# A fused linear-attention and expert kernel: a new hand-fixed instruction order for its first third, with the weight loads' planned transfer times raised

## The chip, the cores and the metric

The kernel runs on one core of one Trainium2 chip. A core has five instruction streams that matter here: TensorE (PE in the profile; its weight loads are listed apart as PEld), VectorE (DVE), ScalarE (ACT), GpSimd (POOL) and SyncE (SP). Each stream runs its instructions in the order in which the program lists them. POOL and SP also start the DMA transfers of this kernel: POOL loads inputs and weights, SP moves an intermediate to and from DRAM and stores the result. The metric is the time of one execution in microseconds of device time, lower is better; the median of three runs before the change is 970.37 us (969.55 to 971.73).

## The reference, cut to what matters

```python
def phi(x): return np.where(x > 0, x, np.exp(x) - 1.0) + 1.0
# attention: q, k, v are (8, 8, 576, 64)
kv  = einsum('bhsd,bhse->bhde', phi(k), v);  z = phi(k).sum(axis=2)
num = einsum('bhsd,bhde->bhse', phi(q), kv)
den = einsum('bhsd,bhd->bhs', phi(q), z)[..., None] + 1e-06
x   = (num / den) as (4608, 512)
# experts: w_gate (512, 8), w1 (8, 512, 1024), w2 (8, 1024, 512)
P = exp(x @ w_gate - max)
for _ in range(8):                      # Sinkhorn
    P /= P.sum(1, keepdims=True) + 1e-09
    P /= P.sum(0, keepdims=True) + 1e-09
    P *= 4608 / 8
out = sum over e of P[:, e:e+1] * (relu(x @ w1[e]) @ w2[e])
```

## The kernel before, in words

The 4608 rows of x are cut into nine groups of 512. Expert e has a first matrix w1(e) and a second matrix w2(e). In the attention part (`att`, sixteen head pairs numbered by n) inputs are loaded by POOL, ACT takes exponentials, DVE builds phi and evicts products, PE multiplies. Into this part the first layers of expert 0 are woven, group by group (`layer1`), and the eight Sinkhorn steps on DVE with one small PE product each (`sinkhorn`, lines 542 to 573). Forty-six products on a zero tile (`f_warm`, line 591) have no use in the result; they stand where PE has nothing else at the start.

From group 4 or 5 of expert 0 on, both layers are computed as two-by-two block products with seven block multiplications instead of eight (`block7` with line 811 for layer one, `unit` with line 1051 for layer two). For each expert these need combinations of blocks of the weights, made by DVE in `combos`: four tasks W from w1 (line 983) and four tasks T from w2 (line 997). Combinations of x per group (`x_blocks`, lines 727 to 732) are stored to DRAM buffers by SP and fetched again for each later expert (`x_load`, line 762). Each output piece is collected in a buffer acc; for expert 0 it is scaled by P afterwards (`scale0`, lines 899 and 901, possible once the last Sinkhorn task is done), for later experts a product is scaled and added as it leaves PSUM (line 1082 on DVE, lines 1089 and 1092 on ACT and POOL).

Weights are loaded by `load_w` (line 316, issued by POOL). There are two buffers for w1 and two for w2. Expert 0 has its w1 in four quarters and its w2 in two halves; for e of 1 and more, w1 comes as two loads of 64 partitions each (512 KB written) and w2 as one load of the whole matrix (1024 KB written). w1(1) and w2(1) may start only after a small POOL instruction (`f_gx`, line 1133) that waits until the x combinations of the first five groups are stored.

The order of all work comes from `_Plan`. Every task has an engine or a choice of engines, a planned duration, dependencies and buffers. `add` numbers the tasks from 0; a transfer is a task of its own on a single server called "dma", with a planned time and a latency, and the x loads and the stores of the x combinations are tasks of that server too. `run` puts out tasks one by one, and the program is what each engine gets in this sequence. The string `_FRONT` fixes the sequence of the first 1733 tasks: a number and a letter for the engine, p for PE, a for ACT, d for DVE, g for POOL, s for SP, m for the transfer server, n for none. After the last token the planner chooses by its own modelled times. So a token's place fixes what an engine has to do first, while on the chip every instruction starts when its semaphores allow it. The i-th instruction of an engine in the trace can be matched with the i-th token of its letter, by counting the instructions that each task issues; that is how task numbers and times are put together in the prediction.

Tasks that are named below: 48, 50, 52 are the loads of k, q, v of head pair 0; 54 to 66 its arithmetic, 58p its first product (line 414); 109, 111, 114, 116 the four quarters of w1(0); 602 to 612 the first layer-one products of expert 0 (line 685); 572, 586, 787, 845 stores of x combinations of groups 2, 4, 5 and 6; 590 is `f_gx`; 592 and 594 the halves of w1(1), 598 the whole w2(1); 1007 to 1010 the W and 1011 to 1014 the T combinations of expert 1; 1018 the first product of expert 1; 1529 and 1531 the halves of w1(2), 1535 w2(2), 1538 to 1545 the combinations of expert 2; 2060 and 2062 the halves of w1(3), 2066 w2(3).

Of the kernel before, what the change touches and what calls it, by code (L numbers as in the profile page):

```python
# [17 lines left out]
class _Plan:  # L18
# [121 lines left out]
    48s 49m 1n 2p 3p 50g 51m 4p 52g 53m 5p 6p 78g 79m 7p 8p 76g 77m 9p 10p 80g 81m 54a 11p 12p 0g 13p 14p 15p 126g 127m  # L140
    16p 17p 18p 128g 129m 19p 61n 62a 63d 130g 131m 55d 56d 154g 155m 64d 57n 108n 58p 109g 110m 20p 59a 21p 22p 89n
    90a 91d 156g 157m 23p 65p 24p 60a 66d 25p 26p 82a 111g 112m 27p 28p 83d 67p 29p 30p 68a 31p 84d 158g 159m 69p 92d
    85n 86p 70a 114g 133d 115m 71a 32p 93p 87d 33p 94d 34p 88a 182g 183m 35p 132a 36p 72p 139n 141d 95p 73d 37p 38p 96a
    39p 116g 117m 134d 74p 140a 97p 40p 75d 41p 42p 184g 185m 98a 161d 135n 136p 160a 142d 43p 186g 187m 44p 137d 143p
    99a 138d 45p 144d 46p 102p 167n 168a 210g 211m 103d 145p 47p 162d 146a 113n 119n 120g 602p 121m 169d 100p 603p 101d
    147p 212g 213m 170d 148a 163n 164p 149a 171p 165d 214g 215m 604p 172d 166a 555g 152p 605p 153d 188a 173p 150p 174a
    151d 118n 606p 106g 107m 608p 189d 601n 607a 175p 240g 241m 610p 609a 195n 197d 612p 176a 242g 243m 190d 614p 196a
    613d 244g 245m 191n 192p 177a 198d 616p 615d 123g 124m 216a 199p 193d 618p 194a 200d 617a 180p 556d 611a 201p 181d
    620p 202a 270g 271m 217d 178p 621a 122n 622p 179d 223n 224a 624p 218d 225d 619a 203p 226d 300g 301m 219n 220p 204a
    562g 205a 227p 221d 639p 222d 228d 246a 206p 641p 207d 638n 640a 104g 105m 229p 247d 642a 208p 268g 269m 643p 209d  # L150
    230a 272g 273m 253n 254a 645p 644d 298g 299m 248d 231p 647p 232a 255d 256d 328g 329m 249n 250p 648a 233a 302g 303m
    257p 251d 125n 625p 326g 327m 258d 252a 646a 236p 281n 283d 259p 237d 623p 260a 632d 282a 234p 261p 235d 649p 262a
    284d 628p 311n 312a 630d 629p 275d 263a 266p 650d 285p 274a 626p 286d 651p 267d 636a 382g 383m 304a 276d 238p 356g
    357m 313d 652a 314d 277n 278p 339n 341d 627p 279a 305d 239a 280a 340a 653p 306d 354g 355m 563d 287p 330g 331m 264p
    288a 657p 265d 384g 385m 289p 634d 358g 359m 307n 308p 290a 333d 557g 332a 315p 309d 659p 310d 654a 316d 442g 443m
    558s 559m 291a 672p 334d 412g 413m 342d 317p 292p 386g 387m 318a 658p 293d 367n 368a 319p 361d 660p 369d 320a 294p
    414g 415m 674p 667a 295d 321a 564g 343p 671n 673d 335n 336p 344d 388a 565s 566m 370d 676p 416g 417m 360a 389d 296p
    390d 496g 497m 337a 655p 362d 297a 338a 675a 345p 395n 397d 322p 346a 678p 323d 665a 347p 576d 324p 348a 661p 325d
    577g 396a 371p 677d 363n 364p 372d 679a 349a 398d 656p 444g 445m 365d 418a 440g 441m 680p 366d 663d 352p 373p 353d
    662p 374a 419d 681a 350p 375p 351d 425n 426a 682p 669d 391n 392p 376a 420d 377a 684p 393d 500g 501m 683d 498g 499m  # L160
    399p 685a 688p 468g 469m 394a 400d 453n 454a 380p 427d 401p 381d 686p 402a 428d 378p 687a 403p 379d 705p 404a 455d
    446a 421n 422p 447d 470g 471m 578d 569g 405a 429p 423d 579s 580m 689p 424d 560s 561m 430a 406p 707p 407d 567s 568m
    510n 511a 472g 473m 431p 456d 408p 690p 505g 432a 409d 704n 708a 691p 448d 706a 503d 433p 449n 450p 434a 570d 696a
    457p 451d 502a 709p 458d 435a 692p 452d 583d 459p 512d 438p 460a 693p 439d 698a 461p 475d 436p 462a 711p 437d 463a
    410p 584d 513d 585g 464p 411a 694p 700a 465d 474a 514p 504d 571g 586s 587m 466p 695p 515a 467d 710d 506n 507p 481n
    482a 572s 573m 712d 574s 575m 713p 476d 508a 509a 702a 741d 715p 581s 582m 714a 483d 516p 742d 477n 478p 517a 716d
    484d 518p 479a 717p 519a 480d 485p 718a 719p 520a 486d 590g 591n 592g 593m 521p 487p 522d 594g 595m 727p 488a 720d
    523p 489p 524d 746p 490a 743d 494p 491a 721p 744d 748p 745n 747a 495d 728p 749d 492p 750p 493d 722p 553n 737d 751a
    784d 525p 729a 738d 785g 752p 526a 735a 528d 725p 753a 754p 786d 554p 755a 739d 527n 529p 787s 788m 756p 588s 589m
    530d 842d 726p 757a 531d 843g 789s 790m 758p 760p 759a 1015s 1016m 723p 761a 762d 792p 532p 724p 740d 793a 733a  # L170
    533d 796p 763d 731a 794p 534d 766p 795a 798p 767a 768p 799a 791n 797a 800p 844d 802p 764d 845s 846m 806p 1072s
    1073m 801d 535p 772p 807a 803d 769a 810p 536d 773a 812p 765d 804p 537d 813a 808p 776p 809a 811a 770p 805a 816p 850p
    817d 774p 851a 777d 771a 814p 596n 1007d 818p 775d 538p 778p 819a 815d 854p 820d 779a 856p 849n 855a 539d 852p 821d
    857a 864p 1008d 826p 865a 822d 853a 866p 900d 824p 540d 901g 860p 825a 870p 827a 828p 867a 871a 830p 861d 874p 902g
    831a 858p 875d 868p 859d 834p 869a 823d 862p 1009d 541p 876p 863a 835d 872p 908p 873d 958g 832p 909a 542d 877a 836p
    833d 829a 878d 910p 837a 912p 911a 922p 879d 907n 913a 914p 959d 882p 543d 915a 923a 924p 918p 925a 928p 883a 884p
    929a 919d 916p 885a 880d 926p 960d 920p 917d 930p 961s 962m 921a 888p 963s 964m 1010d 927a 931d 544p 932p 889a 903s
    904m 966p 933d 905s 906m 892p 967a 881d 934p 545d 847s 848m 893d 972p 935a 890p 546d 973a 886p 968p 887a 970p 969a
    894p 936d 891d 547p 976p 895a 548d 980p 965n 971a 977d 974p 981a 940p 937d 975d 986p 549d 942p 987a 941a 984p 943a
    982p 978p 983a 946p 938d 990p 947a 550p 944p 985a 551d 979a 552d 950p 939d 736a 988p 991d 1018p 896a 948p 951d 780a  # L180
    989d 992p 730a 952p 949d 1528n 1529g 1530m 1019a 1020p 732g 953a 1024p 1006n 1021a 1000p 1025a 734g 1026p 1022p
    1028p 699g 1017n 1023a 998p 1029d 993a 668a 666d 597n 598g 599m 999p 781d 635a 1531g 1532m 1030p 1004d 1001p 1031a
    631g 703d 1032p 1034p 840g 1033a 994p 945d 1005a 637d 1038p 897g 995p 1039a 1027d 1035a 633d 996p 1002a 600n 1011d
    1040p 1036p 1012d 1042p 1037a 1075p 1043d 664a 1077p 1013d 997p 1076a 1078a 1041d 1044p 670a 1014d 1081p 1129s
    1130m 1045a 1083p 1003a 1079p 1046d 1050p 1082a 1047d 1052p 1048d 1051a 1074n 1080a 1055p 1053d 1054d 1085p 1049d
    1058a 1060p 838a 1086d 1059g 1063p 697d 1062d 1061d 1087p 1065d 1089p 955d 1091p 1090a 1066p 1092a 1088a 1095p
    1067d 1097p 1084d 1096a 1093p 1068d 1099p 1094a 782d 1132p 1100d 701a 1134p 1098d 1069p 1133a 1135a 1064d 1101p
    1056a 1071d 1138p 1070d 1102a 1186s 1187m 1057g 1140p 1139a 1103d 1136p 1107p 1104d 1109p 1105d 1108a 1112p 1111d
    1110d 1142p 1106d 1113a 1117p 1131n 1137a 1143d 1120p 1119d 1533n 1538d 1144p 1118d 1146p 1141d 1148p 1147a 1123p
    1149a 1145a 1152p 1124d 1154p 1125d 1153a 1150p 1122d 1156p 1155d 1151a 1189p 1157d 1191p 1190a 1121d 1126p 1192a  # L190
    1158p 1128d 1195p 1127d 1159a 1243s 1244m 1197p 1115a 1160d 1193p 1196a 1164p 1161d 1188n 1194a 1166p 1162d 1165a
    1163d 1169p 1168d 1167d 1199p 1170a 1539d 1174p 1171g 1200d 1177p 1175d 1114g 1176d 1201p 1198d 1203p 1202a 899d
    1205p 1204a 954d 1180p 1178d 1206a 1179d 1209p 1182d 1211p 1181d 1210a 1207p 1213p 1208a 1246p 1214d 1248p 1247a
    1212d 1183p 1249a 1172a 1215p 1185d 1173g 1252p 1184d 1216a 1300s 1301m 1254p 1253a 1116g 1217d 1250p 1221p 1218d
    1223p 1222a 1219d 1226p 1225d 1220d 1256p 1229a 1224d 1231p 1245n 1251a 1230g 1257d 1227a 1234p 839g 1233d 1258p
    1236d 1260p 957g 1232d 1259a 1262p 1540d 1261a 1237p 1263a 841g 1266p 1255d 1268p 1267a 1239d 1264p 1238d 1270p
# [29 lines left out]
def kernel(  # L226
# [28 lines left out]
    add = S_.add  # L255
# [50 lines left out]
    def load_w(ten, nm, pl, pieces, e, prio, deps=(), shape=None):  # L306
        g = S_.grp(pl)
        ts_ = []
# [4 lines left out]
        for part in pieces:  # L313
            for sl, off, ap in part:
# [3 lines left out]
                ti = add(("pool", 0.8), fn, acq=[gsw], use=[g, gsw], prio=prio, deps=[tal, w_part.get(nm) if ts_ else None])  # L318
# [891 lines left out]
```

## Time and profile before

| | |
|---|---|
| median of three runs | 970.37 us (969.55 to 971.73) |
| the profiled execution's own time | 969.86 us |
| its span, first to last instruction | 967.8 us |
| PE busy | 952.0 us, 98% of the span, 8576 products |
| DVE busy | 780.3 us, 81% |
| ACT busy | 578.9 us, 60% |
| POOL busy | 184.7 us, 19% |
| mean granted TensorE clock | 0.996 |
| DMA mean | 116 GB/s |

The span is cut by the page into 40 slices of 24.2 us. "Idle before" is the time in which an engine had nothing to run ahead of an instruction, and the arrow names what ended it. A wait for several things is put down to the one that came last. A DMA is listed where it is issued, and its landing is known from the semaphore that it raises.

### The profile page before, as it was taken

The numbers are of one execution on the slowest core, as the hardware profiler recorded it, in microseconds if no ns is written. First come the engines' busy times: TensorE is split into PE (matmuls) and PEld (weight loads), VectorE is DVE, ScalarE is ACT, GpSimd is POOL, SyncE is SP. The second block draws the span as 40 slices with busy tenths as digits, with TensorE's granted clock in tenths as the row PEclk, the third lists the DMA queues.
The fourth block names the chain that finished last, engine by engine and source line by source line (L and its number), as shares of the span: only waits on it lengthen the run. The fifth ranks groups of instructions, "written<-read, shape, count | busy, mean of one in ns | idle before, by whom it ended". The sixth has DMA issues, their size and how long they took to land.

```text
span 967.8 us, 21113 instructions
## 1 busy us (share of the span) xinstructions
PE 952.0 (98%) x8576; PEld 805.4 (83%) x8576; DVE 780.3 (81%) x1476; ACT 578.9 (60%) x1029; POOL 184.7 (19%) x238
## 2 busy tenths in 40 slices
PE   8999999999999999999999999999999999999998
PEld 4565578678888888888888888888888888888886
DVE  6899899588888788878887888878887888877775
ACT  6899756645555555555555555555555555555553
POOL 6653201401312011111112111111112111111110
PEclk9999999989999999999999999999999999999999
DMA  9999442522253622272226322272226322235554
GB/s 229 242 249 250 121 153 94 79 85 77 77 121 91 151 77 78 79 161 77 75 69 132 102 75 71 74 162 76 76 75 140 102 77 77 78 99 163 165 162 111
DMA packets 45681, 112.52 MB, mean 116 GB/s; under 512 B 4368, under 2 KB 25616, under 8 KB 45584
## 3 DMA queue, kind: packets, MB, share of 16 engines
q1 hardware_dynamic: 21056, 75.57, 23.7%
q0 software_dynamic: 24128, 35.07, 19.3%
q8 instruction: 67, 1.10, 0.5%
q10 hardware_dynamic: 400, 0.52, 0.2%
q14 instruction: 30, 0.25, 0.1%
HBM read 119.69 MB, written 17.69 MB: 142 GB/s over the span
## 4 chain that ended last, share of the span: by engine, by line
PE 78%; DMA 2%; DVE 0%; issue 0%; ACT 0%; ACTq 0%
PE ye L1051 33%; PE hq L811 22%; PE R L811 11%; PE Zye L811 6%; PE Zye L1051 6%; DMA w<-in_moe_w_dram 1%; DMA xs<-xd 1%; PE ye L933 1%; PE yc L917 0%; DVE h L849 0%; ACT st L1089 0%; DVE T L997 0%; DVE acc L1082 0%; DVE acc L922 0%; ACTq L1089 0%
## 5 line engine op out<-in xcount | busy, mean ns | idle before, releaser
L1082 DVE SCALAR_TENSOR_TENSOR acc<-ye,P_sb,acc 128x256 f32<-128x256 f32 x620 | 268.5, 479 | 124.5 <-PE ye L1051 122.8
L811 PEld LDWEIGHTS <-W 128*128 128x128 f16 x2144 | 210.2, 98 | 25.3
L1051 PEld LDWEIGHTS <-S 128*128 128x128 f16 x1984 | 194.1, 98 | 22.5
L1092 POOL TENSOR_TENSOR acc<-acc,st 128x256 f32<-128x256 f32 x124 | 88.1, 730 | 626.0 <-ACT st L1089 608.7
L1051 PE MATMUL ye<-T,S 128*128 128x256 f16 x1488 | 192.8, 273 | 0.0
L811 PEld LDWEIGHTS <-w 128*128 128x128 f16 x1608 | 157.5, 98 | 25.2 <-issue 5.3
L1051 PEld LDWEIGHTS <-h 128*128 128x128 f16 x1584 | 155.3, 98 | 18.4
L846 ACT ACTIVATE h<-hq 128x512 f16<-128x512 f32 x134 | 80.1, 598 | 140.5 <-PE hq L811 136.1
L811 PE MATMUL hq<-xs,W 128*128 128x256 f16 x1008 | 151.7, 273 | 0.0
L811 PE MATMUL R<-xs,W 128*128 128x256 f16 x1008 | 151.7, 273 | 0.0
L811 PE MATMUL hq<-xs,w 128*128 128x256 f16 x1008 | 141.5, 273 | 5.0 <-DVE h L849 4.9
L843 ACT ACTIVATE h<-Zye 128x512 f16<-128x512 f32 x134 | 80.1, 598 | 39.3 <-PE Zye L811 39.3
L826 ACT COPY Zye<-hq 128x512 f32<-128x512 f32 x134 | 77.7, 580 | 36.8 <-PE hq L811 36.8
L1089 ACT ACTIVATE st<-Zye,P_sb 128x256 f32<-128x256 f32 x124 | 53.0, 471 | 70.9 <-PE Zye L1051 70.9
L1022 DVE TENSOR_TENSOR S<-h 128x1024 f16<-128x1024 f16 x124 | 86.0, 694 | 11.1 <-ACT h L846 11.1
L849 DVE CUSTOM_DVE_ANT_0 h<-R,s 128x512 f16<-128x512 f32 x126 | 86.5, 687 | 9.5 <-ACT s L833 9.0
L833 ACT COPY s<-hq 128x512 f32<-128x512 f32 x126 | 73.6, 584 | 33.9 <-PE hq L811 33.2
L849 DVE CUSTOM_DVE_ANT_0 h<-hq,s 128x512 f16<-128x512 f32 x126 | 86.7, 688 | 8.0 <-PE hq L811 7.9
L811 PE MATMUL Zye<-xs,w 128*128 128x256 f16 x504 | 76.1, 274 | 0.0
L840 ACT COPY s<-R 128x512 f32<-128x512 f32 x126 | 74.7, 593 | 0.0
L1051 PE MATMUL ye<-w,h 128*128 128x256 f16 x528 | 69.2, 274 | 0.0
L1051 PE MATMUL Zye<-w,h 128*128 128x256 f16 x528 | 68.4, 272 | 0.0
(126 smaller groups left out, 1011.7 us busy)
## 6 DMA issues: line engine op xcount, KB each, us to landing
xs<-xd SPq DMA_DIRECT2D x63, 896.0 KB, 4.6
kin<-in_k_dram POOLq DMA_DIRECT2D x15, 576.0 KB, 8.4
out_dram<-acc SPq DMA_DIRECT2D x67, 128.0 KB, 2.4
w<-in_moe_w_dram POOLq DMA_DIRECT2D x16, 512.0 KB, 8.7
w<-in_moe_w_dram POOLq DMA_DIRECT2D x7, 1024.0 KB, 13.0
qin<-in_q_dram POOLq DMA_DIRECT2D x16, 288.0 KB, 8.3
vv<-in_v_dram POOLq DMA_DIRECT2D x16, 288.0 KB, 8.2
xd<-acc SPq DMA_DIRECT2D x5, 512.0 KB, 5.1
```

What stands on the lines that cost most here:

```text
L811: nc.tensor.matmul(dst[:, p, :], lhsT=lhs(p, c), rhs=rhs(c), start=(first and p == 0 and c == 0), stop=(c == 1), skip_group_check=True)
L826: nc.scalar.copy(out=Zt[1], in_=gX["tile"])
L833: nc.scalar.copy(out=gs2["tile"], in_=gX["tile"])
L840: nc.scalar.copy(out=gs5["tile"], in_=gR["tile"])
L843: nc.scalar.activation(out=hd(0, 0), in_=Zt[1], func=AF.Relu)
L846: nc.scalar.activation(out=hd(1, 0), in_=gX["tile"], func=AF.Relu)
L849: nc.vector._custom_dve(TENSOR_ADD_SAT, out=dst, in0=ps, in1=sb, s0=3.0e38, s1=0.0)
L1022: nc.vector.tensor_tensor(out=Sx[:, i], in0=a0, in1=a1, op=op)
L1051: nc.tensor.matmul(bank(g_)[:, s, :], lhsT=lhs(s, kk), rhs=rhs(kk), start=(new and s == 0 and kk == 0), stop=(kk == 3), skip_group_check=True)
L1082: nc.vector.scalar_tensor_tensor(out=dst(), in0=bank(g_)[:, s, :], scalar=P_sb[:, gg, e:e + 1], in1=dst(), op0=ALU.mult, op1=ALU.add)
L1089: nc.scalar.mul(out=gst["tile"], in_=bank(g_)[:, s, :], mul=P_sb[:, gg, e:e + 1])
L1092: nc.gpsimd.tensor_tensor(out=dst(), in0=dst(), in1=gst["tile"], op=ALU.add)
```

## The change

Two things are edited. In `load_w` the planned transfer time of one load becomes 1.55 us instead of 1.4 for a quarter of w1(0), stays 2.6 us for half a w1 and for half of w2(0), and becomes 5.4 us instead of 2.6 for a whole w2. And `_FRONT` is replaced by another sequence of 1725 tokens of the same tasks. 83 tasks that stand in both sequences stand on another engine; no task of PE, SP or a load is among them. The computation, the tiles, the buffers and the dependencies are the same, and the file still counts stores on the server of the loads, as it did.

The main moves in the new sequence: 598g (w2(1)) stands straight behind 590g and ahead of 592g and 594g, where it stood behind both of these and nine further POOL tasks: five of x combinations, three of scaling and the first half of w1(2); 594g stands behind three x combinations on POOL (842g, 844g, 901g); 1531g stands in group 4 of expert 1, 1535g in group 1 of expert 1; the combinations of expert 2 (1538d to 1545d) start in group 5 of expert 1 instead of group 1; 586s stands behind 787s; the four quarters of w1(0) and 52g stand earlier, 63d stands behind 55d and 56d. The order of POOL from `f_gx` to w2(2), in tokens:

```
before: 590 592 594 785 843 901 902 958 1529 732 734 699 598 1531 631 840 897 1059 1057 1171 1114 1173 1116 1230 839 957 841 1287 898 1228 1285 1342 1535
after:  590 598 592 842 844 901 594 958 637 957 701 699 1529 898 839 633 1059 666 780 664 896 840 1114 1116 955 841 1535
```

The diff, cut to the lines with tokens that are spoken of:

```diff
-    48s 49m 1n 2p 3p 50g 51m 4p 52g 53m 5p 6p 78g 79m 7p 8p 76g 77m 9p 10p 80g 81m 54a 11p 12p 0g 13p 14p 15p 126g 127m
-    16p 17p 18p 128g 129m 19p 61n 62a 63d 130g 131m 55d 56d 154g 155m 64d 57n 108n 58p 109g 110m 20p 59a 21p 22p 89n
...
-    99a 138d 45p 144d 46p 102p 167n 168a 210g 211m 103d 145p 47p 162d 146a 113n 119n 120g 602p 121m 169d 100p 603p 101d
...
-    484d 518p 479a 717p 519a 480d 485p 718a 719p 520a 486d 590g 591n 592g 593m 521p 487p 522d 594g 595m 727p 488a 720d
...
-    817d 774p 851a 777d 771a 814p 596n 1007d 818p 775d 538p 778p 819a 815d 854p 820d 779a 856p 849n 855a 539d 852p 821d
...
-    1028p 699g 1017n 1023a 998p 1029d 993a 668a 666d 597n 598g 599m 999p 781d 635a 1531g 1532m 1030p 1004d 1001p 1031a
-    631g 703d 1032p 1034p 840g 1033a 994p 945d 1005a 637d 1038p 897g 995p 1039a 1027d 1035a 633d 996p 1002a 600n 1011d
-    1040p 1036p 1012d 1042p 1037a 1075p 1043d 664a 1077p 1013d 997p 1076a 1078a 1041d 1044p 670a 1014d 1081p 1129s
...
-    1110d 1142p 1106d 1113a 1117p 1131n 1137a 1143d 1120p 1119d 1533n 1538d 1144p 1118d 1146p 1141d 1148p 1147a 1123p
...
+    48s 49m 1n 2p 3p 52g 53m 4p 50g 51m 5p 6p 78g 79m 7p 8p 76g 77m 9p 10p 126g 127m 54a 55d 11p 12p 80g 81m 13p 14p
+    128g 129m 56d 108n 109g 110m 57n 58p 0g 15p 130g 131m 16p 17p 18p 19p 20p 21p 61n 62a 63d 154g 155m 22p 23p 24p 25p
...
+    138a 144d 44p 160a 102p 210g 211m 145p 103d 113n 602p 146a 45p 162d 46p 47p 100p 119n 167n 120g 168a 169d 121m 603p
...
+    787s 788m 528d 756p 586s 587m 755a 789s 790m 735a 722p 757a 738d 554p 588s 589m 729a 527n 529p 723p 739d 530d 1015s
+    1016m 724p 740d 531d 758p 760p 759a 725p 761a 762d 792p 532p 794p 793a 590g 533d 597n 598g 599m 726p 763d 795a 731a
+    591n 592g 593m 796p 764d 733a 798p 534d 842g 800p 799a 766p 802p 767a 806p 791n 797a 768p 801d 807a 803d 535p 770p
...
+    1073m 810p 777d 818p 815d 774p 819a 900d 811a 850p 538p 820d 901g 778p 851a 775d 856p 779a 539d 864p 857a 594g 595m
...
+    831a 868p 875d 862p 596n 1007d 834p 863a 823d 827a 876p 1008d 869a 541p 858p 835d 908p 958g 832p 859d 909a 877a
...
+    948p 1010d 1018p 949d 992p 1019a 989d 1020p 635a 952p 1024p 600n 1006n 1011d 1021a 1000p 953a 1025a 1026p 957g 631a
+    1022p 1028p 993a 701g 998p 1017n 1029d 1023a 1027d 1001p 699g 1030p 1005d 1032p 1528n 1529g 1530m 1012d 1034p 1033a
...
+    1152p 1125d 1154p 1124d 1534n 1535g 1536m 1153a 1150p 1141d 732a 1156p 1057g 1189p 1151a 1157d 1191p 1190a 1121d
...
+    1233d 1260p 782d 954g 1262p 1261a 1237p 1263a 1259a 1266p 1531g 1532m 1239d 1268p 1238d 1267a 1264p 1235d 838a
...
+    1371d 1348p 1369d 1346d 1372p 1347d 1374p 1349d 1373a 1376p 1533n 1538d 1375a 1351p 1539d 1377a 1380p 1350d 1352d
...
+    1618p 2062g 2063m 1595d 1620p 1615d 1622p 1621a 1597p 1623a 1619a 1626p 1599d 1628p 1598d 1627a 1624p 1629d 1630p
...
-                ts_.append(add(("dma", (1.4 if nm == "w1" and len(pieces) > 1 else 2.6)), lambda _: None, deps=[ti],
+                ts_.append(add(("dma", 1.55 if nm == "w1" and len(pieces) > 1 else 2.6 if nm == "w1" or len(pieces) > 1 else 5.4), lambda _: None, deps=[ti],
```

## The prediction

> **What bounds the kernel now.** I read the page first, then the waits of PE, then the stretches of time in which PE is not full, and last the order of instructions around the largest wait.
>
> ```profile
> span 967.8 us, 21113 instructions
> ...
> PE 952.0 (98%) x8576; PEld 805.4 (83%) x8576; DVE 780.3 (81%) x1476; ACT 578.9 (60%) x1029; POOL 184.7 (19%) x238
> ...
> PE   8999999999999999999999999999999999999998
> ...
> PEclk9999999989999999999999999999999999999999
> ```
>
> PE is the bound nearly everywhere. The sequence of products is the same work before and after, so the change can only act on PE's idle time (967.8 - 952.0 = 15.8 us, of which about 4 us are the last eviction and store after PE's end) and on the one slice where the granted clock is not full, the eighth. The waits of PE over the whole span:
>
> ```profile
> PE hq L811 <- DVE h L849: 4.9, 2, 4.5
> PE kv_ps L414 <- DVE t L399: 1.5, 1, 1.5
> PE hq L685 <- DMA w<-in_moe_w_dram: 1.3, 2, 0.8
> ```
>
> One wait of 4.5 us is the largest by three times. The sequence of instructions around it, and the chain that ended last, which begins there with the transfer:
>
> ```profile
> 193.87 0.69 DVE L997 TENSOR_TENSOR T<-w 128x1024 f16<-128x1024 f16 x1 [6.42 <-DMA w<-in_moe_w_dram]
> 194.60 0.69 DVE L997 TENSOR_TENSOR T<-w,T 128x1024 f16<-128x1024 f16 x1
> 195.21 0.68 DVE L849 CUSTOM_DVE_ANT_0 h<-hq,s 128x512 f16<-128x512 f32 x1
> 195.81 0.68 DVE L997 TENSOR_TENSOR T<-w 128x1024 f16<-128x1024 f16 x1
> 195.94 1.01 PE L811 MATMUL hq<-xs,w 128*128 128x256 f16 x4 [4.54 <-DVE h L849]
> ```
>
> ```profile
> 183.29 10.56 DMA w<-in_moe_w_dram
> ```
>
> PE waits for DVE's h (token 1043), h stands on DVE behind two T combinations (1011, 1012), and the first of these waits 6.42 us for w2(1), issued by POOL at 183.29 (598) and landed 10.56 us later. The name in PE's wait is DVE, the cause is a late load. The clock beside it (columns: stretch, length, PE busy, granted clock, DMA share, GB/s):
>
> ```profile
> 190.00:192.00 2.00, 1.40 (x9) 1.00 1.11 158
> 192.00:194.00 2.00, 0.00 (x0) 1.00 1.08 196
> ...
> 196.00:197.00 1.00, 1.00 (x6) 0.50 0.00 0
> ...
> 199.00:200.00 1.00, 1.00 (x7) 0.50 0.97 409
> ...
> 201.00:202.00 1.00, 1.00 (x11) 1.00 0.06 16
> ```
>
> After the wait PE runs at half clock until about 200.9, and counts as busy.
>
> **Part 1, w2(1) moved ahead of w1(1).** In the new order 598 is the first load behind `f_gx` (590). `f_gx` waits for the stores of the first five groups. It ran at 107.7; now the store 586 of group 4 stands on SP behind 787, which was issued at 122.0, so `f_gx` comes at about 122.4 + 2.8 (landing of a store issued there) = 125.3. A w2 issued with no other weights in flight took 9.47 us (1535 at 266.16), so w2(1) lands near 136, while 1011 stands behind products that ran at 178.7. The margin is 40 us. The 4.54 us go. What is late next there: the products at 183.0 followed their h by 0.65 us, which is no wait.
>
> The clock loss: the five product groups between 195.94 and 200.92 (1044, 1081, 1083, 1079 and the first of line 1051) took 0.81, 0.85, 0.86, 0.85 and 1.61 us; at full clock the first four take 0.436 and the last 0.873. That is 4.98 - 2.62 = 2.36 us, gone with the wait, since gaps of up to 1.50 us at the start left the clock at 1.00. The Trainium skill, page "TensorE: Matmul & The Clock Gate", section "Part 1: The HAM clock gate", says the array drops to half rate after an idle window of about 3.4 us and needs about as long of busy work to recover. By it the loss would be 3.4/2 = 1.7 us, an estimate from that page, and the sum 0.66 us smaller; the trace shows about 5 us of half clock, and the row decides.
>
> **Part 2, the start.** PE's idle time before 180 is 1.32 (first instruction) and then 1.50 + 0.47 + 0.23 + 0.24 + 0.50 + 0.17 + 0.28 + 0.24 + 0.85 + 0.07 + 0.67 + 0.29 = 5.51 us, from the gap of every product group. The idle-time products on zeros, 13.3 us in all, stay 46. Three of these gaps have an answer in the new order:
>
> - 1.50 at the first product (58): DVE had 63, which waited 4.14 us for q, ahead of 55 and 56. Now 55 and 56 come first (ready at 4.5 + 1.16 + 0.76 = 6.5) and v is issued first, at 1.65, and lands when q did, at 7.21. The thirteen fill products ahead end at 1.32 + 5.2 = 6.5, so 0.7 remain: 0.8 saved. q now lands at 8.6, and its transpose is expected at about 11.5 against 11.0, so the fill products cover that.
> - 0.50 and 0.85 at the first w1(0) products (602, 606). Loads land one after the other here, 1.4 us each (14.37, 15.73, 17.18). The quarters move from place 10, 12, 14, 16 among POOL's loads to 8, 11, 14, 15, so the second and the fourth land 1.4 to 2.4 us earlier, while PE's own work ahead of 602 and 606 shrinks by 0.8 and 0.4: both gaps go, 1.35 saved.
>
> Together 2.15 us. Bounds: all of the 5.51 could go, and nothing could.
>
> **Part 3, the tasks that change engines.** Eleven x combinations go from POOL to DVE and seven the other way, first-layer evictions eleven to DVE and eight to ACT, and so on, 83 in all. Added up with each instruction's own duration (the median row of its kind where it changes engine), up to the first product of expert 1 (1018) DVE has 170.7 us instead of 168.4, ACT 145.2 instead of 145.1, POOL 61.7 instead of 64.9. The cover is DVE's idle time, 11.4 us between 40 and 180, but between 120 and 170 it is only 2.3 us of 50, and 1.3 of the 2.3 us added fall behind the first product of group 4 of expert 0. Lower bound 0 (hidden in the idle time), upper bound 2.3 as PE time. I take 1.3, because DVE is nearly full just there and feeds PE within 0.1 to 1 us at many places.
>
> **Part 4, w1(1) goes back.** With `f_gx` at 125.3 the halves are issued at about 126.5 (592) and, behind 842, 844 and 901 on POOL, at about 142 (594). Before, they landed at 113.7 and 116.2. The first user, W (1007), ran at 139.2 and now stands behind product 862 (149.6 before). Both hang on 900d: on POOL 901 (1.48) and 594 with its landing (5.6 as the first halves took) give 7.1 us; on DVE 820, 775, 539, 902, 821, 540, 822, 861, 873, 875 give 7.7 us. The load is 0.6 us ahead: cost 0, with bounds below. Queued behind 590 on POOL are also 842 and 844; 842 may then end at 129.4 and 844 near 131.5, as before (131.9 on DVE), and the store 845 and the x load 1072 on SP follow then, for a product at 189.5. x load 1015 now meets w2(1) on the DMA engines; its user comes 45 us later.
>
> **Part 5, expert 1 and later.** w2(2) goes from 266 to about 212 and the second half of w1(2) from 184 to about 240, each alone. The combinations of expert 2 press into the last 45 us of expert 1: three W more than before, 3 x 0.6 = 1.8 us of DVE, against 50 - 41.06 = 8.9 us idle per 50 us there. Four more scalings on POOL (15 for 11, 1.57 us each) lie in its idle time. Cost 0 while DVE keeps that idle time; without it, up to 1.8 us. w1(3) and w2(3) no longer meet an x load together (at 308.97 that took 10.08 us instead of 4.45, and PE waited 0.12): 0.12 saved. The raised 5.4 us acts behind the front only through POOL's place for w2 of later experts, and PE has no wait there to gain or lose: 0.
>
> **Sum.** On the profiled execution: 969.86 - 4.54 - 2.36 - 2.15 + 1.3 - 0.12 = 961.99. The median of the runs is 0.51 above that execution, so **962.5 us**. A change within 0.2% (1.9 us) can hardly be told from none.
>
> **Rivals.**
> - *B, the new front loses elsewhere.* DVE's added work turns into waits in full (2.3), the start saves nothing, and combinations of expert 2 cost 1.8: 970.37 - 7.02 + 4.1 = 967.5, and 965.4 where half of it is true. For it: DVE at 9.3 to 9.8 us of 10 between 120 and 170. Against it: ACT and POOL are free to lag.
> - *C, all start gaps go and DVE hides its work.* 970.37 - 7.02 - 5.51 = 957.8; 960.9 is where it meets the forecast. Against it: several of these gaps are waits between neighbours (PE on DVE and back) of 0.2 to 0.5 us.
> - *D, slower: the second half of w1(1) is the new late load.* In place of T, W (1007) stops DVE at about 148, with everything behind it. If 594 takes 12.98 us to land, as the longest quarter in the crowded start did, it is 6.8 us late; PE then loses about 6.8 and 2.36 of clock: 962.5 + 9.2 = 971.7, and 973.8 if the start saves nothing either. There it is slower by 0.2% from a landing time of 11.5 us on (7.02 - 1.3 + 1.94 - 2.36 = 5.3 us late, and 5.6 + 0.6 in time); the 12.03 of 1531 was with w2 in front. For 594 only an x load can be in flight. The Trainium skill, page "DMA: Bandwidth & Descriptors", section "Queues, rings and completion order", says each DMA engine takes turns packet by packet between the queues that have work. By that rule an x load of SP in flight would halve the rate of 594; the 10.08 us of the x load at 308.97 agrees with sharing.
> - *E, the change doesn't do what it says.* w2(1) is still late because `f_gx` is: that needs 40 us more than the 18 that I allow. Or another input of expert 1 is late at the same place, so that PE stops as before: about 970.
>
> **How the numbers follow.** The forecast, 960.9 to 964.3, has a chance of 0.59, B (964.3 to 968.4) 0.19, C 0.09, D 0.09, E 0.04. 962.5 is the middle of the first. The range 960.2 to 967.6 leaves out D, E, most of C and the end of B, some 0.2. Faster by more than 0.2% are the forecast, B and C, 0.87; the same are E and, with a start that saves, 0.02 of D, together 0.06; the rest of D is slower, 0.07.
>
> **What would show it.** In the changed profile: w2(1) issued near 125 and landed by 140; no wait of T (line 997) on a DMA; no wait of PE over 1.5 us behind the start, and the granted clock at 9 in the eighth slice (Part 1). PE's wait at line 414 near 0.7 and at line 685 on w gone (Part 2). DVE's waits small and PE's on DVE between 120 and 180 summing to about 1.3 (Part 3). No wait of W (line 983) on a DMA (Part 4). No wait in 200 to 330 (Part 5). Wrong would make it a wait of line 983 on w, or PE gaps on DVE of several us behind 120.

## The result and the profile after

The changed kernel takes 964.54 us, the median of seven runs (963.9 to 967.64); the kernel before, run beside it, takes 970.37 us (969.55 to 972.65, seven runs). The ratio is 0.9939, with a 95% interval of 0.9925 to 0.9953. The forecast was 962.5 us. The profiled execution of the changed kernel happens to be its longest, 967.64 us, so its trace shows more loss than a usual run has; a second profile of the same kernel (965.11 us, experiment 2) is read beside it.

From the page of the changed kernel: span, busy time, and PE's clock in 40 slices.

```profile
span 965.6 us, 21108 instructions
...
PE 950.3 (98%) x8576; PEld 805.2 (83%) x8576; DVE 782.0 (81%) x1474; ACT 579.3 (60%) x1031; POOL 184.6 (19%) x238
...
PEclk9999999999999999999999999999999999999999
```

The dip of the clock in the eighth slice is gone. The span is 2.1 us shorter: 1.7 us less PE busy time (952.0 to 950.3) and only 0.4 us less waiting. To see why the waiting hardly fell, the waits of PE (what it waited for, us in total, times, longest):

```profile
PE kv_ps L413 <- DMA vv<-in_v_dram: 3.4, 2, 1.9
PE R L556 <- DVE gs L551: 1.9, 1, 1.9
...
PE kv_ps L413 <- DVE xT L498: 1.2, 1, 1.2
```

The wait of 4.5 us for h has left the head of this list, and the waits for w at the first w1(0) products have left the list. (Code lines stand one lower than before: 997 is 996, 811 is 810, 685 is 684, 414 is 413.) A wait for `gs`, the input of the second small Sinkhorn product, has grown from 0.3 to 1.9 us, and one of 1.2 us for `xT` is new. The study turned on these two. By place, PE waited in us:

| PE idle time, us | 1.4 to 36 | 36 to 120 | 120 to 180 | 180 to 210 | later |
|---|---|---|---|---|---|
| before | 4.55 | 0.74 | 0.29 | 4.54 | 0.44 |
| changed, first profile | 5.54 | 2.23 | 1.95 | 0 | 0.44 |
| changed, second profile | 3.38 | 2.76 | 1.96 | 0 | 0.44 |

At the place of the old stall, DVE's instruction T, in the timeline of the changed kernel (start, duration, engine, line, operation, out and in, idle time before and what ended it), has 0.95 us of idle time ahead of it that is put down to its own issue; its load had landed 47 us earlier, at 136.37:

```profile
183.88 0.69 DVE L996 TENSOR_TENSOR T<-w 128x1024 f16<-128x1024 f16 x1 [0.95 <-issue]
```

And PE around the new wait for `gs` (columns: stretch, length, PE busy, granted clock, DMA share, GB/s), with the stretch of the old stall as the last line:

```profile
128.00:130.00 2.00, 0.63 (x5) 1.00 1.00 380
130.00:131.00 1.00, 0.42 (x3) 1.00 1.14 180
131.00:132.00 1.00, 1.00 (x5) 0.54 1.04 144
...
133.00:134.00 1.00, 1.00 (x6) 0.50 1.23 204
...
180.00:205.00 25.00, 25.00 (x200) 1.00 0.26 59
```

The old stall is gone entirely, clock included. A smaller copy of it, a wait of 1.95 us and 3.41 us of half clock (131.07 to 134.49, which costs about 1.7 us), now stands at 130. What made PE wait there is on two engines at once. DVE, then POOL, in the timeline:

```profile
126.88 3.16 DVE L549 TENSOR_TENSOR wt<-P_sb,Rr 128x288 f32<-128x288 f32 x1
130.07 0.45 DVE L551 TENSOR_REDUCE gs<-wt 128x8 f32<-128x288 f32 x1
```

```profile
125.68 1.56 POOL L315 DMA_DIRECT2D w<-in_moe_w_dram  x2 [0.36 <-issue]
127.25 1.17 POOL L726 TENSOR_TENSOR xst<-xT 128x512 f16<-128x512 f16 x1
128.37 1.16 POOL L727 TENSOR_TENSOR xst<-xT 128x512 f16<-128x512 f16 x1
```

DVE is not queueing there: one instruction of 0.67 us (the median of the eight at this line) lasts 3.16 us, and it ends at 130.04, 0.5 us after the second of the two TENSOR_TENSORs of task 842 on POOL (129.53). That gave a theory which the prediction did not have: DVE instructions are held up by POOL's x combinations. The rival is the prediction's own reason, that DVE has too much work. The two ask for opposite edits.

### The profile page after: what moved, and what is told of

Same layout as the page of the kernel before. It is cut to its first block, busy times and chain, and to the rows that moved or that the text cites. A ratio compares the mean times of both kernels' runs of the same rounds, so it can differ in the third digit from the quotient of the medians.

```text
span 965.6 us, 21108 instructions
## 1 busy us (share of the span) xinstructions
PE 950.3 (98%) x8576; PEld 805.2 (83%) x8576; DVE 782.0 (81%) x1474; ACT 579.3 (60%) x1031; POOL 184.6 (19%) x238
## 4 chain that ended last, share of the span: by engine, by line
PE 95%; DMA 2%; DVE 2%; issue 0%; ACT 0%; POOL 0%; DVEq 0%; ACTq 0%; POOLq 0%
PE ye L1050 36%; PE hq L810 24%; PE R L810 12%; PE Zye L810 6%; PE Zye L1050 6%; PE ye L932 4%; PE hq L684 3%; DMA vv<-in_v_dram 2%; PE kv_ps L413 1%; PE att L439 1%; PE att L470 1%; PE num_ps L470 1%; DVE wt L549 0%; PE att L515 0%; PE yw L590 0%
```

## The experiments

Experiments 1 to 4 ran on one chip beside the kernel before (971.36 us, median of eleven runs), experiments 5 to 8 on another beside it again (970.74, median of 29).

### 1. The kernel before, with w2(1) alone moved

```diff
-    484d 518p 479a 717p 519a 480d 485p 718a 719p 520a 486d 590g 591n 592g 593m 521p 487p 522d 594g 595m 727p 488a 720d
+    484d 518p 479a 717p 519a 480d 485p 718a 719p 520a 486d 590g 591n 592g 593m 521p 487p 522d 594g 595m 597n 598g 599m
...
-    1028p 699g 1017n 1023a 998p 1029d 993a 668a 666d 597n 598g 599m 999p 781d 635a 1531g 1532m 1030p 1004d 1001p 1031a
+    1026p 1022p 1028p 699g 1017n 1023a 998p 1029d 993a 668a 666d 999p 781d 635a 1531g 1532m 1030p 1004d 1001p 1031a
```

> The kernel before with one change: the load of w2(1), tokens 597n 598g 599m, stands behind 595m, straight behind both halves of w1(1); nothing else is moved. Theory L (the late load is the whole gain): the T combinations wait for no DMA, PE's 4.54 us wait at line 811 and the 2.36 us of half clock go, and the rest of the new order is worth nothing or costs: 970.4 - 6.9 = 963.5, at most 964 and below the changed kernel. Theory R (the new order as a whole brings it): with the old order around it another input of expert 1 is late next, PE still stops for 1 us or more between 180 and 205, and the time is 965 to 969.

Measured: 963.51 us (961.9 to 964.67, six runs), ratio 0.9915 (0.9898 to 0.9932). w2(1) was issued at 112.61 and landed at 125.16. The head of PE's waits, and DVE where it stopped before:

```profile
PE kv_ps L414 <- DVE t L399: 1.9, 1, 1.9
PE hq L685 <- DMA w<-in_moe_w_dram: 1.7, 2, 1.1
```

```profile
188.85 0.89 DVE L901 TENSOR_SCALAR acc<-acc,P_sb 128x512 f32<-128x512 f32 x1
189.67 0.68 DVE L997 TENSOR_TENSOR T<-w 128x1024 f16<-128x1024 f16 x1
```

T follows its neighbour without a wait, the wait for h is not at the head of the list, PE does not wait at all between 180 and 210, and the mean granted clock is 1.0 instead of 0.996. One load in another place gives 7.85 us (6.6 to 9.9 by the interval); Part 1 had 6.9. It is also more than the whole change gave: no run of it was as long as the shortest run of the changed kernel in experiment 2. So the other moves of the new order, with the load early, cost something.

### 2. The changed kernel once more

No edit.

> The changed kernel once more, for a second profile beside the others. The profile shown was its slowest of seven runs (967.64 against a median of 964.54). Expected: 964.5 again; in the profile the wait for v at 7.9, about 1.6 at 27.7, 1.2 at 95 and 1.9 at 130.6 again, since they come from the order. If the half clock of 3.4 us behind 131 is missing here, it is what parts the slow runs from the others (1.7 us).

Measured: 965.94 us (965.07 to 966.54, six runs), ratio 0.9942 (0.9925 to 0.9959), the same as the first time within the intervals. The wait of 1.96 us for `gs` is there again, at 129.7, but this time PE runs on at full clock. So that wait is a property of the order, and the half clock behind it is not in every run. The wait of 1.18 us for `xT`, at 94.4, also comes again; DVE and then POOL ahead of it:

```profile
90.89 2.76 DVE L450 TENSOR_SCALAR tq<-qin 128x1152 f16<-128x1152 f16 x2
93.57 0.74 DVE L498 TENSOR_TENSOR xT<-num_ps,rden 128x576 f16<-128x576 f32 x1
```

```profile
90.24 1.15 POOL L727 TENSOR_TENSOR acc<-xT 128x512 f16<-128x512 f16 x1
91.34 0.72 POOL L380 DMA_DIRECT2D kin<-in_k_dram  x1
92.08 1.25 POOL L729 TENSOR_TENSOR acc<-xT,acc 128x512 f16<-128x512 f16 x1
```

Two TENSOR_SCALARs last 2.76 us together, beside the x combinations of tasks 583 and 584 and a DMA issue between these, and the eviction of `xT` stands behind them.

### 3. Task 842 on DVE

```diff
-    591n 592g 593m 796p 764d 733a 798p 534d 842g 800p 799a 766p 802p 767a 806p 791n 797a 768p 801d 807a 803d 535p 770p
+    591n 592g 593m 796p 764d 733a 798p 534d 842d 800p 799a 766p 802p 767a 806p 791n 797a 768p 801d 807a 803d 535p 770p
```

> The changed kernel with task 842 (x combinations of group 6, first part) on DVE instead of POOL, in the same place. Theory P (POOL at work stretches a DVE instruction of some forms): the DVE instruction wt<-P_sb,Rr at line 549 near 127 falls from 3.16 us to below 1.2, PE's wait of 1.95 us for the second Sinkhorn product falls below 0.5 although DVE has 0.7 us more to do, and the time is 1.5 to 3 us below the changed kernel, 961.5 to 963. Theory O (DVE has too much in that place): wt stays long or the wait grows by 0.7 us, and the time is 964.5 to 966.

Measured: 962.91 us (961.37 to 964.31, six runs), ratio 0.9909 (0.9892 to 0.9926), 3.0 us below experiment 2. DVE in the timeline:

```profile
126.29 0.67 DVE L549 TENSOR_TENSOR wt<-P_sb,Rr 128x288 f32<-128x288 f32 x1
126.99 0.45 DVE L551 TENSOR_REDUCE gs<-wt 128x8 f32<-128x288 f32 x1
```

DVE was given more to do and was done sooner: the instruction takes 0.67 us, PE waits for nothing between 120 and 180, and DVE's busy time in the whole span falls from 782.1 (experiment 2) to 779.5 us, because the time that an instruction is held up counts as busy. The theory that DVE has too much work asked for the opposite, and falls for this place. Of the 3.0 us the trace explains 1.96 as the wait; the rest may be half clock in the unprofiled runs, whose mean clock is 0.997 to 0.999 in experiment 2 and 0.999 or 1.0 here, but no trace of those runs shows where.

### 4. Tasks 583 and 584 on DVE

```diff
-    448d 429p 423a 472g 473m 424a 686p 430d 405a 583g 406p 687d 705p 453n 454a 407d 431p 691p 455d 432a 468g 469m 510n
-    512d 511a 408p 584g 433p 409d 707p 434a 698d 470g 471m 449n 450p 704n 708a 456d 505g 706d 689p 451a 435a 513d 457p
+    448d 429p 423a 472g 473m 424a 686p 430d 405a 583d 406p 687d 705p 453n 454a 407d 431p 691p 455d 432a 468g 469m 510n
+    512d 511a 408p 584d 433p 409d 707p 434a 698d 470g 471m 449n 450p 704n 708a 456d 505g 706d 689p 451a 435a 513d 457p
```

> The changed kernel with tasks 583 and 584 (x combinations of group 4) on DVE instead of POOL, in the same places. Theory P: the two DVE instructions of line 450 near 92 and 93 fall from 1.45 and 1.40 us to 0.46, PE's wait of 1.19 us at the product of head pair 13 (line 413) falls by half or more although DVE has 1.2 us more: time 0.3 to 1 us below the changed kernel. Theory O: the wait grows by the added work, 2 us or more, and the time is 965 or more.

Measured: 964.16 us (962.76 to 966.46, six runs), ratio 0.9925 (0.9908 to 0.9943), 1.8 us below experiment 2, though the ranges overlap. The same two TENSOR_SCALARs in the timeline:

```profile
92.44 0.82 DVE L450 TENSOR_SCALAR tq<-qin 128x1152 f16<-128x1152 f16 x2
```

From 2.76 us to 0.82, and the wait for `xT` fell from 1.18 to 0.12 us. The mechanism is the same at a second place, with another kind of DVE instruction. (POOL's DMA issues move too, and end ahead of the TENSOR_SCALARs here; where such an instruction met a DMA issue alone it was 0.32 us longer at most, as the last section says.) The profile is that of the longest run. The wait for `gs`, which this edit does not touch, stands in it with 1.95 us up to 129.61, and 3.41 us of half clock follow it; the same stretch of half clock stands at 8.07, at the end of a wait of 2.53 us for v.

### 5. All three tasks on DVE

The edits of experiments 3 and 4 together, on the changed kernel.

> The changed kernel with 583, 584 and 842 all on DVE. If POOL's work beside DVE is the cause of both waits, the two gains add up: PE has neither the wait of 1.2 us near 95 nor that of 1.95 us near 130, and the time is 1 to 1.5 us below the kernel with 842 alone on DVE (962.9 there): 961.4 to 962. If DVE is by then full, it is 963 or more.

Measured: 961.17 us (960.37 to 962.08, four runs), ratio 0.9907 (0.9894 to 0.992). This is faster than both kernels: its interval lies below that of the change (0.9925 to 0.9953), and no run of it is as long as the shortest run of the changed kernel (963.9). From experiment 3 alone (0.9909) it can't be told apart. Its largest waits of PE:

```profile
PE kv_ps L413 <- DMA vv<-in_v_dram: 1.8, 1, 1.8
...
PE att L470 <- ACT rden L483: 0.8, 2, 0.6
```

These lie in the start. Not all of the mechanism is gone: at 52.57 a TENSOR_SCALAR of line 450 takes 2.04 us instead of 0.45 beside a TENSOR_TENSOR of POOL (53.11 to 54.28), as one does in the changed kernel. PE has 0.60 us of idle time shortly behind it, which the profile puts down to a load of v here and to DVE in the changed kernel. DVE is busy for 778.9 us, 3.2 less than in experiment 2, with five instructions more.

### 6. The start of before, the rest as changed

```diff
-    48s 49m 1n 2p 3p 52g 53m 4p 50g 51m 5p 6p 78g 79m 7p 8p 76g 77m 9p 10p 126g 127m 54a 55d 11p 12p 80g 81m 13p 14p
+    48s 49m 1n 2p 3p 50g 51m 4p 52g 53m 5p 6p 78g 79m 7p 8p 76g 77m 9p 10p 80g 81m 54a 11p 12p 0g 13p 14p 15p 126g 127m
...
```

The sequence of before goes up to token 616p; from there on the tokens follow in the new order.

> The changed kernel, but the sequence up to token 616p (about 34 us) is that of the kernel before, and what is left follows in the new order. The start of the changed kernel has had 3.2 to 5.5 us of PE's waits up to 36 us in four profiles, that of the kernel before 4.5 and, with w2(1) early, 6.0. Theory 1 (the new start saves about 1 us, by the quarters of w1(0)): the waits for w at line 685 (0.5 to 1.1 us each) are back, and the time is 0.5 to 1.5 us above the changed kernel run beside it last (965.9): 966.4 to 967.4. Theory 2 (the new start saves nothing, since v lands late): 965 to 966.

Measured: 967.38 us (964.37 to 969.84, twelve runs), ratio 0.9969 (0.9956 to 0.9982). The first waits of PE in its profile, which is that of its shortest run:

```profile
PE R L556 <- DVE gs L551: 2.0, 1, 2.0
PE kv_ps L413 <- DVE t L398: 1.4, 1, 1.4
...
PE hq L684 <- DMA w<-in_moe_w_dram: 1.1, 2, 0.8
```

The waits at lines 413 on `t` and 684 on w, which Part 2 wanted to remove, are back with the old start. The new start removes the waits for w; at the first product of line 413 it puts a wait for v (1.87 and 1.45 us) in the place of that for `t`. How much it is worth is not settled. The medians (967.38 here, 964.54 and 965.94 for the change) would give 1.4 to 2.8 us, the ratios to the kernel before 2.6 to 2.9, but they were not taken side by side. A part is half clock: the clock averages 0.9979 over these twelve runs, and 0.9986 and 0.9983 over the two sets of the change, which by an estimate (difference times span) is 0.4 to 0.6 us. In the profiles PE waits 3.85 to 6.04 us between 1.4 and 36 with the old start (four profiles, mean 4.69) and 3.38 to 5.54 with the new one (six profiles, mean 4.12): 0.6 us, inside the spread.

### 7. The changed kernel, with w2(1) late again

The tokens `597n 598g 599m` move from behind 533d to behind 1024p, ahead of the T combinations.

```diff
-    1016m 724p 740d 531d 758p 760p 759a 725p 761a 762d 792p 532p 794p 793a 590g 533d 597n 598g 599m 726p 763d 795a 731a
+    1016m 724p 740d 531d 758p 760p 759a 725p 761a 762d 792p 532p 794p 793a 590g 533d 726p 763d 795a 731a 591n 592g 593m
...
-    948p 1010d 1018p 949d 992p 1019a 989d 1020p 635a 952p 1024p 600n 1006n 1011d 1021a 1000p 953a 1025a 1026p 957g 631a
+    1018p 949d 992p 1019a 989d 1020p 635a 952p 1024p 597n 598g 599m 600n 1006n 1011d 1021a 1000p 953a 1025a 1026p 957g
```

> The changed kernel with the load of w2(1) (597n 598g 599m) moved back to expert 1, behind product 1024p, one scaling on POOL ahead of it. Theory L: it is issued near 180 and lands some 10 us later, T (line 997 there, 996 here) waits 6 to 9 us, PE stops for 4 to 7 us and runs at half clock for 3.4 or 6.8 us: 6 to 10 us above the changed kernel, 971 to 976. Theory R: another part of the new order keeps PE busy meanwhile, 966 to 969.

Measured: 970.4 us (969.77 to 972.27, ten runs), ratio 0.9997 (0.9986 to 1.0009). The load was issued at 179.77 and landed at 189.3. The waits of all engines between 175 and 205, and DVE's T:

```profile
DVE T L996 <- issue: 7.8, 1, 7.8
...
PE hq L810 <- DVE h L848: 4.1, 1, 4.1
```

```profile
189.57 0.85 DVE L996 TENSOR_TENSOR T<-w 128x1024 f16<-128x1024 f16 x1 [7.82 <-issue]
```

The old stall comes back with its chain (load, T, h, PE), and takes 4.5 to 5.9 us of the gain by the two medians of the change, a little less than was expected. Without the early load the rest of the new order is worth nothing that can be measured. The view names "issue" as what T waited for; that it is the load is read from the landing time, 0.3 us ahead of T.

### 8. The new planned times alone, with the old sequence

```diff
-                ts_.append(add(("dma", (1.4 if nm == "w1" and len(pieces) > 1 else 2.6)), lambda _: None, deps=[ti],
+                ts_.append(add(("dma", 1.55 if nm == "w1" and len(pieces) > 1 else 2.6 if nm == "w1" or len(pieces) > 1 else 5.4), lambda _: None, deps=[ti],
```

> The kernel before, with the new planned times of the loads alone and the old sequence. The fixed part of the order does not read them, so only the order behind it can differ. Expected by both theories: no change, 970 to 971.5 beside a before of 970.4 to 971.4. If it is 1 us or more away, the planner's order behind the front matters.

Measured: 969.42 us (968.53 to 972.34, ten runs), ratio 0.9994 (0.9984 to 1.0005). PE's first wait is the old one:

```profile
PE hq L811 <- DVE h L849: 5.0, 2, 4.7
```

With the old sequence the planned times change nothing that can be measured. What they do behind the new sequence was not tried apart.

## Why the prediction was right, and where it was wrong

**Part 1 held.** `f_gx` ran at 125.22 (125.3 was predicted), w2(1) was issued at 125.68 and landed at 136.37 (near 136), T waits for no load, and PE and its clock are full from 180 to 205. Experiment 1 shows the load alone to be worth 7.85 us, with the 6.9 of this part inside its interval, and experiment 7 takes the gain of the change back. The part took the clock's share as a fixed sum that goes with the wait. Its remark that gaps of up to 1.50 us left the clock alone stands, but a gap of 1.95 us was enough for 3.41 us of half clock in the first profile after. The 2.36 us were one case of a price that differs from run to run: with a like stall, experiments 7 and 8 show 3.41 us of half clock where the profile of before shows 6.83.

**Part 2 held for two gaps of three; its size is open.** PE no longer waits for w at the first w1(0) products, as said. The third gap did not shrink: v landed at 7.81 instead of 7.21, so the first product at line 413 waited 1.87 and 1.45 us in the two profiles of the change instead of the 0.7 that was to remain. In the first profile PE waited 1.58 us for another v at 27.7 (0.2 to 0.4 us at that product in other profiles of this start). The term of 2.15 us measures about 0.6 in PE's waits, inside their spread, while the times of experiment 6 would allow 1.4 to 2.9. Why v lands 0.6 us later than q did in that place was not tried.

**Part 3 is the step that failed.** The term taken was +1.3 with an upper bound of 2.3, both from the work added to DVE, and nothing was charged for where POOL's work lies in time. The waits between 36 and 180 rose by 3.2 us in the first profile (4.18 against 1.03) and 3.7 in the second, beyond the bound, and not from DVE's added work: giving DVE three more tasks took the two large ones away (experiments 3 to 5), and 1.72 us are left there in experiment 5. In place of the step: a task moved to POOL, or left there while a DVE chain moves beside it, can hold up the DVE instructions that it meets, and the cost is what the chain behind them loses. The trace of before had rows of this kind. Line 545's `wt` took 1.41 us instead of 0.45, on DVE and beside it on POOL:

```profile
123.45 1.41 DVE L545 TENSOR_TENSOR wt<-P_sb,cc 128x288 f32<-128x288 f32 x1
```

```profile
123.28 1.26 POOL L730 TENSOR_TENSOR xst<-xT,xst 128x512 f16<-128x512 f16 x1 [3.25 <-DVE xst L727]
```

And at 87.48 a TENSOR_SCALAR of line 395 took 1.71 us instead of 0.75 beside line 728 on POOL, shortly ahead of the gap of 0.67 us that the prediction lists. The step used busy times by engine, and no row of this kind.

**Part 4 held.** 594 was issued at 145.93 and landed at 151.51, 4 us later than said; the W instruction on it ran at 153.34 without a wait. Rival D did not come about.

**Part 5 held in its cost of 0, not in its gain of 0.12.** w2(2) took 12.0 us to land and the x load beside it 8.56, and no PE wait came from either. The wait of 0.12 us for an x load at 319 is gone, but another of 0.12 stands at 296.92, behind a TENSOR_TENSOR of DVE (line 1021) that took 1.58 us instead of 0.68 beside one of POOL (295.56 to 296.30). So PE's idle time behind 210 is 0.44 us before and after.

**The sum.** With Part 2 at 0.6, Part 3 at 3.2 to 3.7 and nothing for Part 5, the prediction's own sum gives 970.37 - 6.9 - 0.6 + 3.2 (or 3.7), which is 966.1 to 966.6; with the 2.15 of Part 2 left in, it gives 964.5 to 965.0. The medians are 964.54 and 965.94, so the sum does not settle Part 2. That the time lies within the stated range is owed to Part 1, which is larger than all the rest together, and to the width of the range (7.4 us); it says nothing for Part 3. The direction rests on Part 1: with the load late again, the rest of the order gains nothing (experiment 7). The 964.54 lies at the border of the forecast's own case and rival B, and in substance it is B: the new front loses elsewhere. B's mechanism was again DVE's added work and the start, so it was right in what it gives and wrong in why. Rivals C and E are excluded by the waits that remain and by T without a wait.

## What to carry to other kernels

When a stall ends at a late load, try that load's place alone first: here it gave 7.85 us, and the other moves that came with it cost about 2.4 us again (experiment 1 against 2). When work moves between VectorE and GpSimd, don't only add up busy time on each; look at which instruction of the one runs beside which of the other, and compare every duration with the median of its line, since an instruction held up is listed as busy and not as waiting. A short wait of PE can cost more than its own length through the clock, and in some runs only, so repeat a profile before a number of this kind goes into a sum.

## What the runs showed of the hardware

**VectorE is held up by GpSimd.** An f32 TENSOR_TENSOR of 128x288 took 3.16 and 3.18 us instead of 0.67 beside two GpSimd TENSOR_TENSORs of 1.17 us, and two f16 TENSOR_SCALARs of 128x1152 took 2.76 us together instead of 0.82. The TENSOR_TENSOR ended when the second GpSimd instruction had ended, not the first. In experiment 7 the same two met a SCALAR_TENSOR_TENSOR of 128x36 (line 547), which took 2.46 us instead of 0.20. A DMA issue of GpSimd alone did little: in experiment 3 GpSimd issues two loads from 125.10 to 126.66, and VectorE's line 549 beside their end (at 126.29) kept its 0.67 us; of the 65 f16 TENSOR_SCALARs of 128x1152 that met only DMA issues in the ten traces, 11 were over 0.1 us longer than their median, by 0.32 us at most.

The Trainium skill, page "SBUF — State Buffer", section "Who interferes with whom", says that VectorE and GpSimd share one pair of ports under an exclusive lock, which a VectorE instruction needs when it has two SBUF inputs (against a GpSimd instruction that reads SBUF) or runs in a two-port mode, as a TENSOR_SCALAR can. The traces agree with the first case, and fit the second; in which mode the TENSOR_SCALARs ran they do not show. The same section says that whichever issues first holds the pair for its whole instruction. By the recorded starts that is borne out in part: of the 20 f32 TENSOR_TENSORs of 128x288 that met a TENSOR_TENSOR of GpSimd in the ten traces, seven began 0.16 to 0.31 us ahead of it and kept their duration, three began 0.02 us behind it and kept it, and six began 0.17 to 0.42 us behind it and were held up. But the four at the wait for `gs` began 0.37 to 0.39 us ahead (126.88 against 127.25 in the first profile) and lost all the same; GpSimd's recorded spans are rough.

**The clock fell after a wait of under 2 us.** The half clock came in pieces of 3.41 us or twice that. It came after the wait of 1.95 us for `gs` in the first profile of the change and in experiment 4, and not after the same wait (1.96 us) in the second profile or in experiment 6; with waits of 4.13 us (experiment 7) and 4.67 us (experiment 8), and for 6.83 us with one of 4.54 us in the kernel before. In the start it came with idle times of 1.97 us (experiment 7) and 2.53 us (experiment 4), and not with 1.93 us in experiment 1. The Trainium skill, page "TensorE: Matmul & The Clock Gate", section "Part 1: The HAM clock gate", gives an idle window of about 3.4 us as the condition and a window of that length until the clock returns. The length agrees (3.41 us), the condition does not: here less than 2 us of idle time were enough in some runs. What decides whether a given run pays it stays open.
